# State update of a chunked linear attention by head: 48-column k v products on their own output partitions, two 48 x 48 quarters of the identity for the state so far

## The chip, the cores and the metric

The kernel runs on one core of a Trainium2 chip. The metric is the device time of one execution in microseconds (us); the median over runs is compared. Five engines work side by side, each through its own list of instructions: TensorE (PE, with its loads of weights as PEld), VectorE (DVE), ScalarE (ACT), GpSimd (POOL) and SyncE (SP), which issues most of the transfers (DMA). TensorE's clock is granted at one of two levels, 2.4 GHz or half of that; the profile gives it as a share of full speed.

## What is computed

Three layers in a row; the change is in the first, a linear attention with a decaying state per head (4 batches, 8 heads, 768 steps, 48 features):

```python
for t in range(S):
    cur = np.einsum('bhd,bhe->bhde', u[None] * kt, vt)
    y[:, :, t] = np.einsum('bhd,bhde->bhe', rt, state + cur)
    state = w[None, :, :, None] * state + np.einsum('bhd,bhe->bhde', kt, vt)
```

Then each of the 3072 tokens goes to one of 8 experts (ReLU, 384 to 1024 to 384), and then through a gated layer (384 to 1536 to 384) behind an RMS norm.

## The kernel before

The attention works on blocks of 128 steps: `n = 0 .. 23` is chunk `c = n // 4` of batch `b = n % 4`. One turn of the main loop is an iteration n. The last chunk (n = 20 to 23) needs no new state; the first (n = 0 to 3) has no old one. PE, DVE and ACT run in the order in which the code is written; the orders of POOL and SP are chosen by a scheduler when the program is built.

On PE an iteration with an old state holds, in this order: `scores(n + 1)` (L322: k by r, 48 features contracted, the two heads of a pair on input partitions 0 to 47 and 64 to 111), `xtrans(n - 1)` (L372), then in `attend(n)` the weighted v of the step itself (L333), r by the state (L335), `logits(n - 1)` (L383), scores by v (L343: 128 weight columns, 48 streamed columns, per head), and the new state (L358, L360). A matmul in float32 is two PE instructions, so the trace counts twice as many as the code writes. In the first chunk L333, L335 and L358 are missing, and L346 stands behind L343. Up to n = 5 a few matmuls of ones (`busy`, L99) are put in between.

The new state is made like this. Two heads share a pair `g` of 96 columns. The k of a block, decayed by `decayk` (L281), lies in one of five buffers `kdb` with each head padded from 48 to 64 columns, the pad zeroed once by POOL (L266). L360 multiplies 112 weight columns of a pair (48 + 16 zeros + 48) by 96 columns of v, so that a 112 x 96 block comes out: two 48 x 48 blocks that are wanted (a head's k by its own v) and two that are not. L358 adds the old state ahead of it, through a 112 x 112 identity. L363 on DVE multiplies by `w128`, which holds the decay over 128 steps for the wanted blocks and zero for the others; `w128` is made once from `pw` and a mask of two columns `hm` (L243, L244, L530).

The routing of the tokens (`route`) runs once per four blocks in pieces; the second piece begins on PE with L439, between L335 and L383, and waits for `cums`, the last of a row of small DVE instructions (L408 to L427) that begins one iteration earlier.

The loads of a block to come are issued by SP; that of v waits until L360 of the block that used the buffer is done (four buffers).

Of the kernel before, what the change touches and what calls it, by code (L numbers as in the profile page):

```python
# [7 lines left out]
F32 = mybir.dt.float32  # L8
# [5 lines left out]
ALU = mybir.AluOpType  # L14
AX = mybir.AxisListType

P = 128
# [7 lines left out]
HP = 64  # L25
# [21 lines left out]
def bcast(ap, shape):  # L47
    return ap.to_broadcast(shape)
# [3 lines left out]
def fused_kernel(  # L52
# [130 lines left out]
    with tc.tile_pool(name="at1", bufs=1) as at1, \  # L183
# [58 lines left out]
        hm = at1.tile([PP, 2], F32, name="hm")  # L242
        nc.vector.tensor_scalar(hm[:, 0:1], pidx[:PP], float(D), None, op0=ALU.is_lt)  # L243
        nc.vector.tensor_scalar(hm[:, 1:2], pidx[:PP], float(HP), None, op0=ALU.is_ge)  # L244


# [17 lines left out]
        kdb = [at1.tile([P, H, HP], F32, name=f"kdb{i}") for i in range(5)]  # L264
        for t in kdb:
            nc.gpsimd.memset(t[:, :, D:], 0.0)  # L266
# [11 lines left out]
        def decayk(n):  # L278

            kd[n] = kdb[n % 5]  # L280
            (nc.vector if n < 2 else nc.gpsimd).tensor_tensor(  # L281
                kd[n][:, :, :D], rkin[n][:, DM:].rearrange("p (h d) -> p h d", h=H), ftab, op=ALU.mult)
# [44 lines left out]
        def attend(n, between):  # L327
# [25 lines left out]
            if c < NCH - 1:  # L353
                s = st[b] if c > 0 else at1.tile([PP, G, PD], F32, name=f"s{b}")
                sf = s.rearrange("p g e -> p (g e)")
                if c > 0:

                    nc.tensor.matmul(pkv[:PP, :DM], ident[:PP, :PP], sf, start=True, stop=False, skip_group_check=True)  # L358
                for g in range(G):
                    nc.tensor.matmul(pkv[:PP, g * PD:(g + 1) * PD],  # L360
                                     kd[n].rearrange("p h d -> p (h d)")[:, g * 2 * HP:g * 2 * HP + PP],
                                     vv[:, g * PD:(g + 1) * PD], start=(c == 0), stop=True, skip_group_check=True)
                nc.vector.tensor_tensor(sf, pkv[:PP, :DM], w128.rearrange("p g e -> p (g e)"), op=ALU.mult)  # L363
                st[b] = s
# [163 lines left out]
        w128 = at1.tile([PP, G, PD], F32, name="w128")  # L528
        for j in range(2):
            nc.vector.tensor_tensor(w128[:, :, j * D:(j + 1) * D],  # L530
                                    bcast(pw[:, 7, :].unsqueeze(2), [PP, G, D]),
                                    bcast(hm[:, j:j + 1].unsqueeze(1), [PP, G, D]), op=ALU.mult)
# [633 lines left out]
```

## Time and profile before

| what | value |
|---|---|
| median of 3 runs | 923.24 us (922.04 to 928.17) |
| the profiled execution | 925.68 us, its span 923.9 us |
| PE busy | 892.5 us, 97% of the span |
| DVE busy | 505.1 us, 55% |
| ACT busy | 350.8 us, 38% |
| POOL busy | 278.5 us, 30% |
| TensorE clock granted, mean | 0.972 |

The attention takes the first 200 us or so of the span, and the rest is the two layers behind it. PE's share of busy time is high all through, and its matmuls overlap each other, so the share alone does not say which instruction is worth what. For that the chain of work that ended last is read, in which an entry reaches from its own start to the start of the next entry.

### The profile page before, as it was taken

Reading aid. Unit: us, or ns where it says so; the run is one execution under the profiler, and the core shown is the slowest. Engines: PE = TensorE matmul, PEld = TensorE weight load, DVE = VectorE, ACT = ScalarE, POOL = GpSimd, SP = SyncE. Lnnn points to the kernel's source line nnn. Section 1 sums busy time; section 2 is a strip of 40 time slices with the busy share of each in tenths; the row PEclk is TensorE's granted clock in tenths of the full one; section 3 lists DMA queues with packets and bytes.
Section 4 is the critical chain, followed back from the end, with each engine's and each line's share of the span. In section 5 each row is a group of like instructions: output and inputs, shape, how many; then the busy total and the mean of one; then the engine's idle time right before and its main releaser. Section 6 shows DMA issues by size and latency. Waiting matters only on the chain.

```text
span 923.9 us, 12722 instructions
## 1 busy us (share of the span) xinstructions
PE 892.5 (97%) x4912; PEld 783.3 (85%) x4912; DVE 505.1 (55%) x887; ACT 350.8 (38%) x742; POOL 278.5 (30%) x250
## 2 busy tenths in 40 slices
PE   7899999979999999999999999999999999999997
PEld 4788888848999999998878778888888888888886
DVE  6457798755677777877579843422432242233102
ACT  1435546544444544455443422322322142241211
POOL 6446697630000000103312132132123123124121
PEclk8789979988999999999999999999999999999999
DMA  6579866444675566533321000000000000000000
GB/s 181 156 234 284 252 198 198 137 154 131 203 244 180 188 203 209 178 126 104 137 69 50 19 35 1 1 16 19 0 1 35 1 1 35 1 0 35 1 1 34
DMA packets 34263, 93.55 MB, mean 101 GB/s; under 512 B 4368, under 2 KB 12584, under 8 KB 34200
## 3 DMA queue, kind: packets, MB, share of 16 engines
q1 hardware_dynamic: 23976, 53.53, 18.9%
q0 software_dynamic: 8928, 33.83, 11.4%
q10 hardware_dynamic: 1296, 5.35, 1.5%
q8 instruction: 39, 0.64, 0.3%
q14 instruction: 24, 0.20, 0.1%
HBM read 73.19 MB, written 19.50 MB: 100 GB/s over the span
## 4 chain that ended last, share of the span: by engine, by line
PE 80%; DVE 9%; issue 4%; ACT 3%; DMA 2%; POOL 1%; SPq 0%; POOLq 0%; DVEq 0%; ACTq 0%
PE ph L955 11%; PE px L343 5%; PE p2o L619 4%; PE p2o L617 4%; PE p2o L618 4%; PE pg L618 4%; PE pv L619 4%; PE pv L617 4%; PE pv L618 4%; PE pg L619 4%; PE pg L617 4%; PE po L617 4%; PE po L618 4%; PE po L619 4%; PE pa L322 3%
## 5 line engine op out<-in xcount | busy, mean ns | idle before, releaser
L1061 POOL TENSOR_TENSOR l<-sg,h 128x512 fp32r<-128x512 f32 x69 | 92.2, 1336 | 305.2 <-ACT h L1060 303.8
L1051 DVE TENSOR_TENSOR sg<-sg,pv 128x512 f32<-128x512 f32 x72 | 49.4, 686 | 236.7 <-PE pv L619 224.2
L619 PE MATMUL p2o<-hi_o,l 128*128 128x384 f32 x276 | 93.4, 338 | 3.2 <-POOL l L1061 3.2
L1050 ACT ACTIVATE sg<-pg 128x512 f32<-128x512 f32 x72 | 42.9, 596 | 139.7 <-PE pg L619 137.4
L617 PE MATMUL p2o<-hi_o,h 128*128 128x384 f32 x276 | 93.2, 338 | 1.3 <-ACT h L1060 1.3
L618 PE MATMUL p2o<-lo_o,h 128*128 128x384 f32 x276 | 92.7, 336 | 0.0
L1060 ACT CAST h<-sg 128x512 fp32r<-128x512 f32 x69 | 42.9, 621 | 130.7 <-DVE sg L1051 130.7
L617 PE MATMUL pv<-nh,hi_v 128*128 128x512 f32 x216 | 85.3, 395 | 0.9 <-ACT sg L1050 0.9
L618 PE MATMUL pg<-nl,hi_g 128*128 128x512 f32 x216 | 85.1, 394 | 0.5 <-DVE nl L904 0.5
L619 PE MATMUL pv<-nh,lo_v 128*128 128x512 f32 x216 | 85.2, 395 | 0.0
L618 PE MATMUL pv<-nl,hi_v 128*128 128x512 f32 x216 | 85.2, 395 | 0.0
L617 PE MATMUL pg<-nh,hi_g 128*128 128x512 f32 x216 | 85.2, 394 | 0.0
L619 PE MATMUL pg<-nh,lo_g 128*128 128x512 f32 x216 | 85.1, 394 | 0.0
L120 POOL DMA_DIRECT2D raw_w<-in_w_dram x25 | 19.0, 760 | 180.9 <-DVE hl L957 83.7
L955 PE MATMUL ph<-xh,hi_w 128*128 128x432 f32 x192 | 70.3, 366 | 1.8 <-DVE hl L957 1.4
L955 PE MATMUL ph<-xh,lo_w 128*128 128x432 f32 x192 | 69.8, 364 | 0.0
L955 PE MATMUL ph<-xl,hi_w 128*128 128x432 f32 x192 | 69.5, 364 | 0.0
L617 PE MATMUL po<-hh,hi_w 128*128 128x432 f32 x192 | 69.5, 362 | 0.0
L619 PE MATMUL po<-hh,lo_w 128*128 128x432 f32 x192 | 68.8, 358 | 0.0
L618 PE MATMUL po<-hl,hi_w 128*128 128x432 f32 x192 | 68.8, 358 | 0.0
L137 DVE TENSOR_TENSOR lo_w<-raw_w,hi_w 128x768 fp32r<-128x768 f32 x54 | 49.3, 955 | 19.9 <-ACT hi_w L133 19.9
L617 PEld LDWEIGHTS p2o<-hi_o,h 128*128 128x128 f32 x276 | 51.8, 188 | 5.3 <-ACT h L1060 2.1
(208 smaller groups left out, 1890.7 us busy)
## 6 DMA issues: line engine op xcount, KB each, us to landing
raw_w<-in_w_dram POOLq DMA_DIRECT2D x25, 768.0 KB, 5.4
rkTb<-in_rkt_dram SPq DMA_DIRECT2D x48, 192.0 KB
rk<-in_rkv_dram SPq DMA_DIRECT2D x24, 384.0 KB
raw_w<-in_w_dram SPq DMA_DIRECT2D x7, 768.0 KB
xs<-zt ACTq DMA_DIRECT2D x6, 770.0 KB
v<-in_rkv_dram SPq DMA_DIRECT2D x24, 192.0 KB
craw_g<-in_m2g_dram SPq DMA_DIRECT2D x9, 512.0 KB
craw_v<-in_m2v_dram SPq DMA_DIRECT2D x9, 512.0 KB
```

What stands on the lines that cost most here:

```text
L120: ld = self.queue.dma_start(raw.rearrange("p (a n) -> p a n", a=src.shape[1]), src)
L137: eng.tensor_tensor(lo[:, t], raw[:, t], hi[:, t].bitcast(F32), op=ALU.subtract)
L322: nc.tensor.matmul(pas[j][:, g, :], kT[n][t, g, :], rT[n][t, g, :], start=True, stop=True)
L343: nc.tensor.matmul(px[:, h * D:(h + 1) * D], am[n][:, h, :], vv[:, h * D:(h + 1) * D], start=(c == 0 and h == 0), stop=(c > 0), skip_group ...
L617: nc.tensor.matmul(ps, a[0], b[0], start=first, stop=False)
L618: nc.tensor.matmul(ps, a[0], b[1], start=False, stop=False)
L619: nc.tensor.matmul(ps, a[1], b[0], start=False, stop=last)
L955: nc.tensor.matmul(ph[:, :CAP], wp[:, o:o + P], xp[:, i, :CAP], start=(j == 0), stop=(j == len(parts) - 1))
L1050: nc.scalar.activation(sg, pg, AF.Silu)
L1051: nc.vector.tensor_tensor(sg, sg, pv, op=ALU.mult)
L1060: nc.scalar.copy(hh, sg)
L1061: (nc.vector if kept else nc.gpsimd).tensor_tensor(hl, sg, hh.bitcast(F32), op=ALU.subtract)
```

## The change

The five `kdb` buffers lose their pads, and POOL's five memsets of them go. Each head gets its own matmul: 48 weight columns by 48 streamed columns, written to output partitions 0 to 47 for the first head of a pair and 64 to 111 for the second. The result of a block is 48 partitions by 4 x 48 columns for each half, 192 columns where there were 384. The old state is added by two matmuls of a 48 x 48 quarter of the identity, on input and output partitions 0 to 47 and 64 to 111, with 192 streamed columns each. DVE multiplies each half by the decay, read from `pw` with a step of zero, and writes only the wanted blocks of the state; the unwanted blocks are zeroed once, by four memsets of 112 x 384 on POOL. `hm` and `w128` are gone.

```diff
-        hm = at1.tile([PP, 2], F32, name="hm")
-        nc.vector.tensor_scalar(hm[:, 0:1], pidx[:PP], float(D), None, op0=ALU.is_lt)
-        nc.vector.tensor_scalar(hm[:, 1:2], pidx[:PP], float(HP), None, op0=ALU.is_ge)
...
-        kdb = [at1.tile([P, H, HP], F32, name=f"kdb{i}") for i in range(5)]
-        for t in kdb:
-            nc.gpsimd.memset(t[:, :, D:], 0.0)
+        kdb = [at1.tile([P, H, D], F32, name=f"kdb{i}") for i in range(5)]
+
+        states = [at1.tile([PP, G, PD], F32, name=f"s{b}") for b in range(B)]
+        for t in states:
+            nc.gpsimd.memset(t, 0.0)
+        halves = [(slice(j * HP, j * HP + D), slice(j * D, (j + 1) * D)) for j in range(2)]
...
-                kd[n][:, :, :D], rkin[n][:, DM:].rearrange("p (h d) -> p h d", h=H), ftab, op=ALU.mult)
+                kd[n], rkin[n][:, DM:].rearrange("p (h d) -> p h d", h=H), ftab, op=ALU.mult)
...
-                s = st[b] if c > 0 else at1.tile([PP, G, PD], F32, name=f"s{b}")
-                sf = s.rearrange("p g e -> p (g e)")
+                s = st[b] if c > 0 else states[b]
+                kv = pkv[:, :G * D].rearrange("p (g e) -> p g e", g=G)
                 if c > 0:
 
-                    nc.tensor.matmul(pkv[:PP, :DM], ident[:PP, :PP], sf, start=True, stop=False, skip_group_check=True)
+                    for r, e in halves:
+                        nc.tensor.matmul(kv[r], ident[r, r], s[r, :, e], start=True, stop=False, skip_group_check=True)
                 for g in range(G):
-                    nc.tensor.matmul(pkv[:PP, g * PD:(g + 1) * PD],
-                                     kd[n].rearrange("p h d -> p (h d)")[:, g * 2 * HP:g * 2 * HP + PP],
-                                     vv[:, g * PD:(g + 1) * PD], start=(c == 0), stop=True, skip_group_check=True)
-                nc.vector.tensor_tensor(sf, pkv[:PP, :DM], w128.rearrange("p g e -> p (g e)"), op=ALU.mult)
+                    for j, (r, e) in enumerate(halves):
+                        nc.tensor.matmul(kv[r, g, :], kd[n][:, 2 * g + j, :],
+                                         vv[:, (2 * g + j) * D:(2 * g + j + 1) * D],
+                                         start=(c == 0), stop=True, skip_group_check=True)
+                for r, e in halves:
+                    nc.vector.tensor_tensor(s[r, :, e], kv[r], bcast(pw[r, 7, :].unsqueeze(2), [D, G, D]), op=ALU.mult)
...
-        w128 = at1.tile([PP, G, PD], F32, name="w128")
-        for j in range(2):
-            nc.vector.tensor_tensor(w128[:, :, j * D:(j + 1) * D],
-                                    bcast(pw[:, 7, :].unsqueeze(2), [PP, G, D]),
-                                    bcast(hm[:, j:j + 1].unsqueeze(1), [PP, G, D]), op=ALU.mult)
```

On PE, an iteration of the third chunk, before (from the transposes of `xtrans` to the next iteration's scores; `x4` stands for four matmuls in a row):

```order
L372 MATMUL pxT_1143<-ident,x_930 128x128 x3
L333 MATMUL px_1150<-qv_1097,ident 128x384
L335 MATMUL px_1150<-s_522,rkTb_114 128x96 x4
L383 MATMUL pxT_1143<-wr,xT_1147 128x16 x3
L343 MATMUL px_1150<-v_785,am_1048 128x48 x8
L358 MATMUL pkv_1179<-s_522,ident 112x384
L360 MATMUL pkv_1179<-v_785,kdb_189 112x96 x4
L322 MATMUL pa_0_1221<-rkTb_112 128x128
```

The same place in the change, whose line numbers differ by a few:

```order
L373 MATMUL pxT_1198<-ident,x_967 128x128 x3
L331 MATMUL px_1205<-qv_1146,ident 128x384
L333 MATMUL px_1205<-s_193,rkTb_114 128x96 x4
L384 MATMUL pxT_1198<-wr,xT_1202 128x16 x3
L341 MATMUL px_1205<-v_816,am_1097 128x48 x8
L357 MATMUL pkv_1234<-s_193,ident 48x192 x2
L360 MATMUL pkv_1234<-v_816,kdb_186 48x48 x8
L320 MATMUL pa_0_1282<-rkTb_112 128x128
```

Nothing moves past anything else there: one matmul of 384 columns becomes two of 192, and four of 96 become eight of 48, in the same place.

On DVE, from the masking of the first block's scores to the first new state, before (`am` are masked scores, `q` sums of r u k, `rkTb` the decayed r and k by feature):

```order
L324 TENSOR_TENSOR am_213<-pa_1_215,smask 128x4x128
L527 TENSOR_TENSOR pw<-pw 112x4
L530 TENSOR_TENSOR w_228<-pw,hm 112x4x48 x2
L534 TENSOR_SCALAR iota_231<-rowi 128x8
L536 MEMSET cum_233 128x4
L281 TENSOR_TENSOR kdb_188<-rk_146,ftab 128x8x48
L293 TENSOR_REDUCE q_246<-ru_236 128x8
L309 TENSOR_TENSOR rkTb_113<-rkTb_113,decays 112x1024
L324 TENSOR_TENSOR am_265<-pa_0_266,smask 128x4x128
L324 TENSOR_TENSOR am_265<-pa_1_267,smask 128x4x128
L363 TENSOR_TENSOR s_312<-pkv_298,w_228 112x384
```

The same stretch in the change:

```order
L322 TENSOR_TENSOR am_213<-pa_1_215,smask 128x4x128
L528 TENSOR_TENSOR pw<-pw 112x4
L530 TENSOR_SCALAR iota_228<-rowi 128x8
L532 MEMSET cum_230 128x4
L279 TENSOR_TENSOR kdb_185<-rk_146,ftab 128x384
L291 TENSOR_REDUCE q_243<-ru_233 128x8
L307 TENSOR_TENSOR rkTb_113<-rkTb_113,decays 112x1024
L322 TENSOR_TENSOR am_262<-pa_0_263,smask 128x4x128
L322 TENSOR_TENSOR am_262<-pa_1_264,smask 128x4x128
L364 TENSOR_TENSOR s_190<-pkv_295,pw 48x4x48 x2
```

The two products that made `w128` are gone, and the update of the state is two instructions of 48 x 192 where it was one of 112 x 384; the rest stands as it stood.

## Rows read from the trace of the kernel before

**Rows 1.** Busy us by stretch: length, PE, PEld, DVE, ACT, POOL, clock, DMA share, GB/s

```profile
17.00:53.00 36.00, 33.18 (x221) 27.46 (x221) 15.21 (x24) 13.15 (x51) 17.57 (x18) 0.74 0.48 144
53.00:122.00 69.00, 69.00 (x602) 61.36 (x601) 53.37 (x109) 37.10 (x135) 42.54 (x35) 1.00 0.83 254
122.00:142.00 20.00, 19.22 (x127) 16.64 (x128) 16.09 (x33) 8.93 (x30) 15.53 (x15) 0.74 0.65 202
```

**Rows 2.** Chain that ended last, iteration 11 (start us, us, what)

```profile
101.14 1.09 PE pa L322 x16
...
102.71 0.65 PE px L333 x2
...
104.82 1.81 PE px L343 x16
106.64 0.70 PE pkv L358 x2
107.34 0.77 PE pkv L360 x8
108.11 1.09 PE pa L322 x16
```

**Rows 3.** The same chain in the first chunk and at half clock

```profile
21.69 0.78 PE pkv L360 x8
...
39.44 1.47 PE pkv L360 x8
...
129.26 1.39 PE pkv L358 x2
130.64 1.47 PE pkv L360 x8
132.11 2.01 PE pa L322 x16
...
141.90 1.09 PE pa L322 x16
...
161.85 1.22 PE pkv L358 x2
```

**Rows 4.** Groups of PE by form, first 225 us

```profile
L360 PE MATMUL pkv<-v,kdb 128*112 128x96 f32 x160 | 22.4, 292 | 0.0
...
L358 PE MATMUL pkv<-s,ident 112*112 112x384 f32 x32 | 15.1, 555 | 0.0
```

**Rows 5.** PE's instructions at 101 us and at 230 us (start us, us, instruction)

```profile
100.68 0.46 PE L360 MATMUL pkv<-v,kdb 128*112 128x96 f32 x3
101.06 0.38 PE L322 MATMUL pa<-rkTb 48*128 48x128 f32 x2
...
229.72 0.36 PE L918 MATMUL pt<-ident,xg 108*4 108x54 f32 x4
230.01 0.47 PE L617 MATMUL po<-hh,hi_w 128*128 128x432 f32 x1
```

**Rows 6.** Groups of DVE by form, first 225 us

```profile
L324 DVE TENSOR_TENSOR am<-pa,smask 128x512 f32<-128x512 f32 x48 | 30.9, 684 | 6.1 <-PE pa L322 5.7
...
L363 DVE TENSOR_TENSOR s<-pkv,w 112x384 f32<-112x384 f32 x20 | 11.1, 557 | 38.8 <-PE pkv L360 38.8
```

**Rows 7.** All engines in order of time, before the first iteration

```profile
10.72 0.99 POOL L287 TENSOR_TENSOR ru<-rk,ub 128x384 f32<-128x384 f32 x1 [4.33 <-DMA ub<-in_u_dram]
...
13.57 3.57 PE L99 MATMUL pa<-ones 128*128 128x512 bf16 x8 [3.48 <-DVE am L324]
```

**Rows 8.** All engines in order of time, a routing's counts and PE behind them

```profile
95.00 0.36 DVE L427 TENSOR_TENSOR cums<-cums,ohb 128x8 bf16<-128x8 bf16 x2
...
96.97 0.18 PE L439 MATMUL prk<-cums,ones 128*128 128x32 bf16 x1
...
125.92 0.18 PE L439 MATMUL prk<-cums,ones 128*128 128x32 bf16 x1 [0.78 <-DVE cums L427]
```

**Rows 9.** Who waited for whom from 53 to 115 us (us in total, times, longest)

```profile
DVE s L363 <- PE pkv L360: 12.0, 7, 3.6
```

## The prediction

> **What bounds the kernel now.** I read the busy times by stretch first. From 53 to 122 us PE is busy in all 69 us at the full clock, while DVE has 53.4 us, POOL 42.5, ACT 37.1, and the DMA engines a share of 0.83 [rows 1]. PE is the limit of that stretch, but two resources stand close behind it. In the stretches around it (17 to 53, 122 to 142) the granted clock is 0.74, so part of the time PE ran at 1.2 GHz.
>
> Then the chain that ended last, which tells what a PE instruction is worth. In a steady iteration it is PE alone from scores to scores: 101.14 to 108.11, or 6.97 us [rows 2]. The state takes 0.70 us (L358) and 0.77 us (L360) of it, together 1.47. At half clock the same two take 1.39 and 1.47 [rows 3]. L360 stands there 20 times (160 instructions by 8) and L358 16 times (32 by 2) [rows 4]. So at most some 30 us of the kernel's 925 can be touched.
>
> What sets a PE instruction's time shows in three rows of the iteration. L333 streams 384 columns in 0.325 us, 0.85 ns a column. L343 streams only 48 but loads 128 weight columns, and takes 0.113 us, 0.88 ns a weight column. L360 has 112 weight columns and 96 streamed, and takes 0.096 us, that is the larger of 0.098 and 0.082, not their sum [rows 2]. So the time is the larger of loading and streaming. L322 loads and streams 128 columns and should take 0.109 by that, yet 16 of them take 1.09 us, 0.068 each [rows 2]: the two heads, which use different input partitions (0 to 47, 64 to 111), run at the same time.
>
> **The change, part by part.**
>
> *L360, new.* 16 instructions per block, each 48 weight columns (0.042 us) and 48 streamed (0.041). In a row they take 16 x 0.042 = 0.67 us; if the two output halves run in pairs, 0.34. The trace of before has no two matmuls on different output partitions side by side. Its nearest row for a thin output is L918 (4 output columns, 54 streamed): four start at 229.72 and the next matmul at 230.01, so 0.073 each at most with the change of shape behind them in it [rows 5]. That shows that thin instructions can follow each other this fast. The bounds are 0.34 and 0.67. I take 0.34, because the row nearest to it is L322, where halves of the array do run in pairs.
>
> The Trainium skill ("TensorE: Matmul & The Clock Gate", Part 3, Measured speedup vs the span model) gives 2.38 times for three column tiles of 32. Two tiles by the same share would have 1.59 times, an estimate from that page: 0.42 us for L360 and 0.41 for the old state, and with the changes of shape below a gain of 0.46 per block instead of 0.62. No row here shows it.
>
> *Old state, new.* Four instructions of 192 streamed columns: 0.163 each, 0.65 in a row, 0.33 in pairs (both input and output halves differ), against 0.70 now. I take 0.33.
>
> *Changes of the array's shape.* From L360 to L322 the last three L360 take 0.38 us to the next start, where three take 0.29 otherwise [rows 2, 5]: 0.09 for going from the whole array to halves. Before, an iteration has two such changes (into and out of L322). The new one has two more, into the quarters and from them to the column halves: +0.18.
>
> So a block at full clock takes 0.34 + 0.33 + 0.18 = 0.85 instead of 1.47: -0.62, and +0.03 if nothing runs in pairs. At half clock by the same columns (L360's 0.184 for 96 streamed gives 0.092; L358's 0.695 for 384 gives 0.35): 8 x 0.092 + 2 x 0.35 + 0.2 = 1.64 instead of 2.86, -1.2 [rows 3]. In the first chunk three blocks go from 1.47 to 0.94 and one from 0.78 to 0.52, with two more changes of shape as well: -1.85. Of the 16 blocks with an old state, two were at half clock in this trace, at 129.26 and 161.85 [rows 3]. The sum: 14 x 0.62 + 2 x 1.2 + 1.85 = 12.9 us off PE.
>
> *DVE, per block.* One product of 384 columns took 0.557 us; the 512 of L324 take 0.684, so 1.0 ns a column and 0.17 fixed [rows 6]. Two of 192 cost 0.73: +0.17. What hides it: DVE waited 12.0 us for L360 in seven of the nine iterations from 53 to 115 [rows 9]. If that cover were gone, the masked scores queued behind it would be 0.17 late per block, 3 us in all. Below nothing isn't possible, since two instructions replace one of the same length.
>
> *The start.* `w128` and `hm` go from DVE, but PE is covered there by eight matmuls of ones, 3.57 us from 13.57 [rows 7]; gain zero. POOL's memsets change from 5 small ones to 4 of 384 columns, ahead of an idle 4.33 us that ends with a transfer [rows 7]: zero. POOL's order also swaps two products of the first blocks, in the same cover; without it the first weighted v would be 1 us late, once. The product of k in `decayk` has the same 384 elements.
>
> *What comes back.* PE now reaches a routing's L439 earlier by two blocks' gain, 1.24 us. At 96.97 the counts had been ready since 95.36, 1.6 us ahead; at 125.92 PE waited 0.78 us for them [rows 8]. DVE's row starts from PE's own logits and so moves too, but not where DVE is full. I charge one such wait, +1.2. And behind that wait the clock fell: the iteration from 132.11 to 141.90 took 9.79 us instead of 6.97, and its neighbours share it [rows 1, 3]. The new iteration has the same waits with less work between them. I charge one more iteration at half clock, +2.8. The DMA share of 0.83 at 6.97 us an iteration becomes 0.91 at 6.35; since the loads are issued an iteration or more ahead, I charge nothing.
>
> So 12.9 - 4.0 = 8.9 us: the profiled 925.7 becomes 916.8. That execution is 2.4 us above the median of the runs, 923.24; for a median I state 915.0.
>
> **The rivals.**
>
> *A, the forecast:* the halves run in pairs and the chain keeps most of the gain. Speaks for it: L322. 908 to 921 by one or two half-clock iterations more or fewer than charged. Chance 0.60.
>
> *B, the change doesn't do what it says:* two column halves are served one after the other. Then a full-clock block is +0.03, a half-clock one 1.47 + 1.4 + 0.2 against 2.86, +0.2, and the first chunk up to +0.2 per block, together about +1.5: 925 as a median. For it: no row has two column halves together; L322's pairs differ in input partitions, these don't. Chance 0.20.
>
> *C, in pairs, but the time goes elsewhere:* the shorter iteration meets the routing on DVE (routing iterations fill DVE: 16.1 of 20 us from 122 to 142) and the clock falls in three iterations more than before, two above the one charged, with one more wait: 915 + 2 x 2.8 + 1.2 = 922. For it: the clock stood at 0.74 on both sides of the dense stretch [rows 1]. Against it: at 53 to 122 there is no wait at all. Chance 0.13.
>
> *D, slower:* the loads of weights are not hidden any more, so that each thin instruction pays loading plus streaming: 16 x 0.083 + 4 x 0.205 + 0.18 = 2.33 instead of 1.47, +0.86 in 16 blocks, and about +0.8 in the first four: +17, or 940. It decides from about 0.6 us per block on, i.e. if more than two thirds of a load stays bare. Against it: L360 now hides its streaming behind its loads (0.096, not 0.18). The Trainium skill ("TensorE: Matmul & The Clock Gate", Part 3, What overlaps and what doesn't) says that a load overlaps matmuls in flight only where the row groups differ; by that rule D would hold, since the column halves share all rows. The trace of before speaks against the rule, by the same L360, whose instructions share all rows too. Chance 0.05.
>
> **How the numbers follow.** The runs and the comparison tell about 1% from no change, which is 9.2 us, so "faster" means below 914.0. A's own range is cut there a little below its middle: 0.33 faster, 0.27 same. B (0.20) and nearly all of C (0.13) are the same. D (0.05) and 0.02 for something not thought of are slower. Faster 0.33, same 0.60, slower 0.07. The range reaches down to a little below A's end (907, fewer half-clock iterations than before) and up to B's end with the spread of the runs (928).
>
> **What would show it.** In the profile after, the chain's entries for the new L357 and L360 at full clock: 0.42 and 0.43 with the changes of shape, if A; 0.75 each, if B; above 0.9 and 1.4, if D. The steady iteration of 6.97 would be 6.35 under A and C, 7.0 under B. C shows in the granted clock from 122 to 180 us and in waits of PE for `cums`. DVE's update would be two instructions near 0.36 us. The forecast is wrong if the entries of the state are short and the end is still not earlier: then the gain went into waits or the clock, and if pairs don't form at all, its main term is gone.

## The result and the profile after

The change made the kernel slower: median 935.76 us (933.75 to 956.21, 6 runs) against 922.64 us (917.32 to 930.23, 6 runs) of the kernel before, a ratio of 1.0148 with an interval of 1.0100 to 1.0196. The forecast was 915.0 us with a range up to 928, so it was wrong in sign and in range. (Ratios here leave out executions in which the chip was disturbed; medians contain them.)

| | before | change |
|---|---|---|
| profiled execution | 925.68 us | 936.19 us |
| its span | 923.9 us | 934.2 us |
| TensorE clock granted, mean | 0.972 | 0.949 |
| span times mean clock | 898.0 us | 886.6 us |
| span less that | 25.9 us | 47.6 us |

The last two rows are worked out, and they are the key to the case. Span times mean clock is the span as it would be if the same time on PE's clock had all passed at 2.4 GHz; I call it clocked time. It fell by 11.4 us. What is left, the time that the lower level cost, rose by 21.7. The difference of the two is the 10.3 us by which the span grew. Clocked time is not pure work: over 113 executions of the kernel before it runs from 893 to 902 us, and falls by some 0.23 us for each us that the lower level cost (an estimate, a line laid through these executions). By that, 5 of the 11.4 us would come with the lower clock alone.

First the work itself. PE in order of time, in a steady iteration of the change (start us, us, instruction). L357 is the old state, L360 the k v products, L320 the scores of the next block:

```profile
105.98 0.53 PE L357 MATMUL pkv<-s,ident 48*48 48x192 f32 x4
106.44 0.56 PE L360 MATMUL pkv<-v,kdb 128*48 128x48 f32 x16
106.93 1.16 PE L320 MATMUL pa<-rkTb 48*128 48x128 f32 x16
```

From start to start the state takes 0.46 + 0.49 = 0.95 us where it took 1.47 [rows 2]. Steady iterations, from scores to scores, go from 6.97 to 6.45 us, by the same 0.52. At half clock the same two took:

```profile
126.45 0.88 PE L357 MATMUL pkv<-s,ident 48*48 48x192 f32 x4
127.26 0.88 PE L360 MATMUL pkv<-v,kdb 128*48 128x48 f32 x16
128.07 2.08 PE L320 MATMUL pa<-rkTb 48*128 48x128 f32 x16
```

0.81 + 0.81 = 1.62 us, where it was 2.86 [rows 3]. On DVE the update of the state is two instructions of 0.354 us (groups of DVE by form, the first 225 us; busy us, then mean ns):

```profile
L364 DVE TENSOR_TENSOR s<-pkv,pw 48x192 f32<-48x192 f32 x40 | 14.2, 354 | 36.6 <-PE pkv L360 36.2
```

Now the clock. Both kernels cut at the same places of the program: start, scores of block 1, scores of block 6, scores of block 21, first matmul of the experts, end. Columns are length, PE, PEld, DVE, ACT, POOL, clock, DMA share, GB/s. Before:

```profile
0.00:17.10 17.10, 11.01 (x47) 4.49 (x47) 12.59 (x44) 2.04 (x5) 10.77 (x20) 0.84 0.80 207
17.10:58.90 41.80, 38.98 (x268) 32.66 (x267) 17.46 (x26) 16.65 (x64) 18.35 (x18) 0.78 0.54 162
58.90:171.80 112.90, 111.89 (x925) 98.76 (x924) 91.46 (x184) 57.94 (x206) 81.17 (x67) 0.94 0.77 233
171.80:212.40 40.60, 32.09 (x243) 24.76 (x242) 23.29 (x105) 19.56 (x64) 16.12 (x15) 0.88 0.40 130
212.40:923.90 711.50, 698.52 (x3437) 622.66 (x3437) 360.31 (x530) 254.60 (x404) 152.06 (x130) 1.00 0.22 73
```

The change:

```profile
0.00:16.60 16.60, 11.40 (x45) 4.61 (x45) 12.32 (x41) 2.20 (x6) 10.25 (x19) 0.90 0.84 208
16.60:60.90 44.30, 41.28 (x310) 32.73 (x309) 17.98 (x29) 16.32 (x64) 19.05 (x19) 0.69 0.51 151
60.90:176.70 115.80, 111.42 (x1078) 97.02 (x1076) 96.91 (x199) 58.05 (x207) 77.19 (x66) 0.87 0.74 229
176.70:222.50 45.80, 36.69 (x243) 28.66 (x241) 25.37 (x105) 19.48 (x64) 15.41 (x15) 0.76 0.36 115
222.50:934.20 711.70, 700.28 (x3437) 624.63 (x3437) 360.62 (x530) 254.73 (x404) 152.12 (x130) 0.99 0.22 73
```

Length times one less the clock gives what the lower level cost in each stretch: first blocks 9.2 before and 13.7 now; dense stretch 6.8 and 15.1; last blocks and routing 4.9 and 11.0; the rest, by difference from the totals, 5.0 and 7.8. The loss grew in every stretch but the start (2.7 us before, 1.7 now), and two of them have new waits.

In the last blocks, whose PE instructions the change does not touch, the same work takes 5.2 us more. What moved there is the order of POOL, which the scheduler chose anew: the change has the last block's product r u k (L286) behind scatters of routed tokens (L499). POOL and DVE in order of time, and below the dots PE:

```profile
183.80 1.01 POOL L499 DMA_INDIRECT xs<-x,pos  x1 [9.63 <-ACT x L490]
...
188.80 1.00 POOL L286 TENSOR_TENSOR ru<-ru,rk 128x384 f32<-128x384 f32 x1
189.83 0.55 DVE L291 TENSOR_REDUCE q<-ru 128x8 f32<-128x384 f32 x1 [1.88 <-POOL ru L286]
...
195.78 0.91 PE L331 MATMUL px<-qv,ident 128*128 128x384 f32 x2 [0.97 <-ACT qv L300]
```

Before, the same product stood ahead of these scatters:

```profile
174.22 2.08 POOL L288 TENSOR_TENSOR ru<-ru,rk 128x384 f32<-128x384 f32 x1
```

DVE waits 1.88 us for the late product, ACT 3.04 us for DVE's row behind it, and PE 0.67 and 0.97 us for ACT; the scores by v behind that wait take 3.54 us, at half clock, where before, with no such wait, they took 1.91.

The dense stretch also has new idle time: PE is idle for 4.4 us of it (115.80 less 111.42), before for 1.0. One wait is the largest. All engines in order of time, at 111 us of the change:

```profile
111.61 1.28 POOL L151 TENSOR_TENSOR lo_w<-raw_w,hi_w 128x512 fp32r<-128x512 f32 x1
111.86 4.01 DVE L307 TENSOR_TENSOR rkTb<-rkTb,decays 112x1024 f32<-112x1024 f32 x1
112.83 1.00 POOL L279 TENSOR_TENSOR kdb<-rk,ftab 128x384 f32<-128x384 f32 x1
113.80 0.98 POOL L285 TENSOR_TENSOR ru<-rk,ub 128x384 f32<-128x384 f32 x1
114.86 1.86 POOL L286 TENSOR_TENSOR ru<-ru,rk 128x384 f32<-128x384 f32 x1
...
115.97 2.17 PE L320 MATMUL pa<-rkTb 48*128 48x128 f32 x16 [2.51 <-issue]
```

DVE's product of the decayed r and k (L307), 1.21 us at its shortest, takes 4.01 while POOL runs product after product; it ends at 115.87, and PE's scores, which read it, start 0.1 us later after 2.51 idle. POOL is held too: its last product takes 1.86 us there, against 0.98 to 1.03 for the others of that size. The profile names no releaser ("issue"), so this reading was a guess at that point, and was tested.

### The profile page after: what moved, and what is told of

Read it like the earlier page. It is cut to its first block, busy times and chain, and to the rows that moved or that the text cites. A ratio compares the mean times of both kernels' runs of the same rounds, so it can differ in the third digit from the quotient of the medians.

```text
span 934.2 us, 13133 instructions
## 1 busy us (share of the span) xinstructions
PE 901.1 (96%) x5104; PEld 787.7 (84%) x5104; DVE 513.2 (55%) x903; ACT 350.8 (38%) x742; POOL 274.0 (29%) x249
## 4 chain that ended last, share of the span: by engine, by line
PE 67%; DVE 5%; issue 3%; ACT 2%; DMA 1%; POOL 1%; POOLq 0%; SPq 0%; ACTq 0%; DVEq 0%
PE ph L951 11%; PE pg L614 5%; PE pv L615 4%; PE pv L613 4%; PE pv L614 4%; PE pg L615 4%; PE p2o L615 4%; PE pg L613 4%; PE p2o L613 4%; PE p2o L614 4%; PE po L613 4%; PE po L615 4%; PE po L614 4%; PE pt L912 1%; DVE oraw L663 1%
```

## The experiments

Theory 1: the change saves PE what was forecast, and the clock takes back more, for two reasons: PE's time holds less that keeps the clock up, and DVE, stretched by POOL, makes PE wait. Its rivals: the pairs are to blame, for the clock or by their shape; or PE has simply too little to do; or DVE has too much work for shorter iterations. Summary (span and clock are those of the profiled execution, and not given for two kernels):

| kernel | median us | ratio to before (interval) | span, clock, clocked time |
|---|---|---|---|
| the change | 935.76 | 1.0148 (1.0100 to 1.0196) | 934.2, 0.949, 886.6 |
| e1, both fillers | 924.92 | 1.0026 (0.9988 to 1.0064) | 918.0, 0.974, 894.1 |
| e2, thin fillers | 976.73 | 1.0513 (1.0476 to 1.0551) | 979.1, 0.907, 888.0 |
| e3, pairs apart | 936.24 | 1.0140 (1.0088 to 1.0192) | 933.7, 0.956, 892.6 |
| e4, before, both fillers | 922.63 | 0.9972 (0.9941 to 1.0004) | |
| e5, middle filler | 937.48 | 1.0153 (1.0061 to 1.0245) | 933.3, 0.954, 890.4 |
| e6, e5 + first chunk | 937.50 | 1.0134 (1.0044 to 1.0223) | 933.6, 0.958, 894.4 |
| e7, e5 + k decay on DVE | 924.86 | 1.0032 (0.9988 to 1.0075) | 927.8, 0.954, 885.1 |
| e8, e5 + column halves | 930.48 | 1.0032 (0.9991 to 1.0073) | 927.7, 0.959, 889.7 |
| e9, k decay on DVE | 933.63 | 1.0178 (1.0116 to 1.0239) | 924.2, 0.960, 887.2 |
| e10, e1 + e6 + e7 | 921.96 | 1.0027 (0.9985 to 1.0069) | 919.0, 0.972, 893.3 |
| e11, before, k decay on DVE | 920.31 | 1.0008 (0.9960 to 1.0056) | 918.4, 0.977, 897.3 |
| e12, e11 + first chunk | 914.91 | 0.9939 (0.9902 to 0.9976) | 913.8, 0.981, 896.4 |
| e13, change, r u k left out | 924.06 | 1.0007 (0.9944 to 1.0071) | 915.8, 0.965, 883.7 |
| e16, e13 + k decay on DVE | 919.49 | 0.9951 (0.9906 to 0.9996) | 916.7, 0.965, 884.6 |
| e14, e10 + more in the first chunk | 914.62 | 0.9905 (0.9859 to 0.9952) | 907.2, 0.987, 895.4 |
| e15, before + first chunk | 914.48 | 0.9925 (0.9893 to 0.9957) | 913.5, 0.983, 898.0 |
| e17, e14 + column halves | 920.01 | 0.9869 (0.9817 to 0.9920) | |
| e18, e17, middle filler only | 911.27 | 0.9865 (0.9826 to 0.9903) | 909.6, 0.981, 892.3 |

### What holds the clock: e1, e2, e4

Both kernels put matmuls of ones (512 columns, L99) ahead of the scores and in the middle of scores by v, up to block 5. e1 does so up to block 19; e2 puts a float32 matmul of one streamed column at the same places; e4 is e1's edit in the kernel before.

```diff
-            busy(..., NBUSY[4] if n < NFILL else 0)
+            busy(..., NBUSY[4] if n < NT - B else 0)
...
-                if h == H // 2 and n < NFILL:
+                if h == H // 2 and c < NCH - 1:
```

> The change, with the two matmuls of ones (128 x 512, 0.21 us each at full clock) that stand in the first six iterations put into all twenty that make a state: one ahead of the scores, one in the middle of scores by v. Clock theory (the change takes busy work out of PE, and the granted clock falls more often and stays down longer): the time at half clock in the attention falls from some 58 us to below 40, and the time from 936 to 920 to 930, although PE gets 6 us of extra work. Waiting theory (PE is held by VectorE's late products of r and k by the decay, and the clock is only a follower): the long waits ahead of the scores (0.4, 2.5, 1.5 us) stay or shrink a little, the extra work adds up to 6 us, 934 to 942.

> The change, with the same two places filled from iteration 6 on by a thin float32 matmul each (128 weight columns loaded, one column streamed, two instructions, about 0.21 us), so that an iteration is as long as in the filled kernel but PE streams nothing more. Clock theory: no help, the clock falls as often or more often, 936 to 946. Waiting theory: VectorE gets 0.4 us more per iteration, the waits shrink, same as the filled kernel within 3 us.

> The kernel before, with the same two matmuls of ones in all twenty iterations: the control for the filled kernel. Clock theory: half-clock time falls here too, from some 37 us to 25 or less, 915 to 923. Waiting theory: 6 us of extra work, 923 to 930.

Busy times by stretch of e1:

```profile
53.00:122.00 69.00, 67.23 (x690) 57.35 (x689) 60.28 (x113) 35.29 (x129) 45.15 (x38) 0.98 0.84 264
122.00:177.00 55.00, 54.76 (x573) 47.03 (x572) 51.62 (x116) 34.16 (x120) 43.19 (x37) 1.00 0.62 194
```

and of e2:

```profile
53.00:122.00 69.00, 69.00 (x564) 59.65 (x564) 38.54 (x89) 25.95 (x94) 27.47 (x26) 0.72 0.70 220
122.00:177.00 55.00, 55.00 (x376) 47.25 (x374) 28.93 (x69) 21.32 (x71) 32.26 (x28) 0.59 0.44 128
```

In e2 PE is busy in all of both stretches and waits for nothing, and yet the clock stands at 0.72 and 0.59; filled with wide matmuls it stands at 0.98 and 1.00, with 1.8 us of waits in the first. So "PE has too little to do" falls. e1 has 7.5 us more clocked time than the change and is 11 us faster. Not all of that is the fillers': with e1's edit the scheduler puts POOL's last products ahead of the scatters again, the waits in the last blocks are gone, and these lose 4.6 us to the lower level instead of 11.0. In the dense stretch, where both kernels wait, the loss goes from 15.1 to 2.2. In the kernel before the same fillers buy nothing that can be told from no change (e4): from 53 to 122 us it stood at 1.00 already [rows 1].

Filling is not free: steady iterations are 6.92 us in e1, 0.47 above the change, so nearly all of the saving is spent on holding the clock. The filler in the middle alone costs 0.15 of it (6.60, e5).

### Are the pairs to blame: e3, e8

e3 writes the eight products of the first half, then those of the second, so that neighbours share output partitions:

```diff
-                for g in range(G):
-                    for j, (r, e) in enumerate(halves):
+                for j, (r, e) in enumerate(halves):
+                    for g in range(G):
```

> The change, with the eight k v products in another order: the four heads of the first output half, then the four of the second, so that neighbours share their output partitions. If neighbours on different output halves do run in pairs in the change, the 16 instructions take about 0.7 us instead of 0.36 and the steady iteration 6.8 instead of 6.45 us. Clock theory: PE is busy with more of its time again, fewer falls, 925 to 934. Waiting theory: the longer iteration gives VectorE 0.35 us, about the same, 928 to 936. If the pairs are not what shortens the iteration: 6.45 again, 936.

PE in order of time, in e3:

```profile
104.77 0.53 PE L357 MATMUL pkv<-s,ident 48*48 48x192 f32 x4
105.22 0.78 PE L360 MATMUL pkv<-v,kdb 128*48 128x48 f32 x16
105.93 1.16 PE L320 MATMUL pa<-rkTb 48*128 48x128 f32 x16
```

The products take 0.71 us apart and 0.49 in pairs, so pairs are real and worth 0.22 us a block, less than the 0.33 that I gave them. The time of the kernel is the same as the change's: 6 us more clocked time (892.6), a higher clock (0.956), no gain and no loss.

e8 (with the middle filler of e5, as e6 and e7) makes the old state by pieces of the identity that span all 112 input partitions, so that the array goes from column halves to column halves:

```diff
-                        nc.tensor.matmul(kv[r], ident[r, r], s[r, :, e], ...)
+                        nc.tensor.matmul(kv[r], ident[:PP, r], s[:, :, e], ...)
```

> The kernel with one filler, and the old state added by column halves of the identity with all 112 rows (two matmuls of 112 x 48 weights) instead of 48 x 48 quarters, so that one change of the array's shape per iteration goes. If a change of shape costs 0.09 us: the steady iteration is 0.09 us shorter than with one filler, 6.57 us, and 1 to 1.5 us in all. If the quarters' pairs need the separate rows: the old state takes 0.65 instead of 0.33 us, the iteration 6.9, and 4 to 6 us slower.

```profile
85.87 0.53 PE L357 MATMUL pkv<-s,ident 112*48 112x192 f32 x4
86.23 0.53 PE L360 MATMUL pkv<-v,kdb 128*48 128x48 f32 x16
86.69 1.16 PE L320 MATMUL pa<-rkTb 48*128 48x128 f32 x16
```

0.36 + 0.46 = 0.82 where the change has 0.95: the quarters cost 0.13 us a block that column halves don't. Steady iterations go from 6.60 (e5) to 6.47. The Trainium skill ("TensorEngine Tiling (Array Packing)", Key Properties) says that a change of the tiling mode drains the engine; this agrees with it in kind. The median went from 937.48 to 930.48, more than the 2 us of work, but the intervals overlap (1.0061 to 1.0245 and 0.9991 to 1.0073), so the two are not surely told apart.

### Fillers in part, and where k is decayed: e5, e6, e7, e9, e11

e5 has only the middle filler, up to block 19. e6 adds to it, in the first chunk, two fillers ahead of the logits and one more in the middle. e7 adds to e5 that VectorE decays every k, at the end of an iteration. e9 does that alone, without fillers, and e11 in the kernel before.

```diff
-            (nc.vector if n < 2 else nc.gpsimd).tensor_tensor(
+            nc.vector.tensor_tensor(
...
-                if n != -2:
+                if n in (-3, -1):
                     decayk(n + 3)
...
+            if 2 < n + 2 < NT:
+                decayk(n + 2)
```

> The change, with only one of the two extra matmuls of ones, that in the middle of scores by v (128 x 512, 0.21 us), in all twenty iterations that make a state; ahead of the scores it stands in the first six as before. The steady iteration should be 6.66 us, between the change (6.45) and both fillers (6.92). If PE's streaming around the scores by v is what the clock hangs on: no fall in the dense stretch but behind waits, and 919 to 926, 4 us under the two fillers at best. If one filler is not enough: falls as in the change, 928 to 938.

> The kernel with one filler, and in the first chunk (iterations 0 to 3, at half clock for most of the time in every kernel so far) more of them: two in the middle, and two in front of the logits, where PE waits 0.57 us for the transposed block anyway. Clock theory: the first four iterations go from some 9.3 us to 6.5 to 7.5 us each at full clock, 6 to 10 us faster than with one filler alone, 910 to 918. If those iterations are held by something other than the clock: no gain, or 2 us slower for the extra work.

> The kernel with one filler, and the product of k and the decay of all blocks on VectorE at the end of the iteration (0.55 us each) instead of on GpSimd (1.0 us each). It asks whether VectorE's late product of r and k by the decay (up to 4.0 us instead of 1.2 when GpSimd runs without a break) is what PE waited for. If so: those products take 1.2 to 2.0 us, the waits ahead of the scores (2.5, 1.5 us in the change, 1.8 us with two fillers) go, and the time is 2 to 6 us below that of one filler. If VectorE is simply full: its extra 0.55 us per iteration makes the waits longer, 2 to 6 us above.

> The change with the decayed k of all blocks made on VectorE, at the end of an iteration, and no filler (the run with the middle filler and the same move gained 12.6 us on the one without it). Theory 1, GpSimd's products of the size 128 x 384 stretch VectorE's product of r and k, so PE waits for its scores and the clock falls behind that wait: the waits at 116.0 and 167.3 us of the change (2.5 and 1.5) are below 1 us, span times granted clock stays that of the change (886.6), the clock rises from 0.949 to 0.963 or more, the time is 920 to 925. Theory 2, the clock falls for the thin pairs alone, whatever PE waits for: as the change, 932 to 938, clock 0.95.

> A control: the kernel before with the decayed k on VectorE. Theory 1: its PE waits only 0.8 us for VectorE between 53 and 180 us, so there is little to win, span times clock stays 897, clock 0.972 to 0.978: 917 to 924. Theory 2, the move itself is worth the 12 us that it brought the changed kernel, whatever the state does: 908 to 914.

e5 gains nothing on the change. Its dense stretch has waits still (1.62 us at 123.3 for a routing's counts, with two iterations at or near half clock behind), but lost only 5.4 us there. The larger loss of the profiled execution is in the last blocks, 22.0 us (clock 0.61 from 165.9 to 222.4), where the one wait of PE from 166 us to the fall is of 0.21 us. e6 and e7 show the same (20.9 and 22.7 us); what brings it on stays open. e6 clears the first chunk (iterations 2 and 3 take 7.25 and 6.74 us where e5 has 9.03 and 11.45); besides the last blocks it loses 8.0 us in the dense stretch, most of it behind a wait of 3.40 us. Its rows, DVE and PE in order of time:

```profile
118.27 3.78 DVE L428 TENSOR_TENSOR ohb<-oh,m 128x32 bf16<-128x32 f32 x1
...
123.53 0.18 PE L442 MATMUL prk<-cums,ones 128*128 128x32 bf16 x1 [3.40 <-DVE cums L430]
```

A product of 32 elements, 0.19 us otherwise, took 3.78 while POOL ran three products from 118.83 to 121.99. e7's median is 12.6 us below e5's (the intervals overlap a little, 1.0061 and 1.0075), and I took POOL's product of k for the culprit, although the product of r and k still took up to 2.94 us in e7, not 2.0 as expected. e9 says no: with the same move and no filler the change stays at 933.63. Its rows at 119 us:

```profile
119.02 2.85 DVE L426 TENSOR_TENSOR ohb<-oh,m 128x32 bf16<-128x32 f32 x1
...
119.58 1.29 POOL L151 TENSOR_TENSOR lo_w<-raw_w,hi_w 128x512 fp32r<-128x512 f32 x1
...
128.49 2.17 PE L320 MATMUL pa<-rkTb 48*128 48x128 f32 x16 [2.03 <-issue]
```

The product of r and k takes 2.02 us at most in e9, so that much the move did. But a routing's product is held while POOL runs the weight split (above) and r u k: the row is 2.7 us late, what is queued behind it too, and PE waits 2.03 us at the scores. So e9's waits (2.03 and 1.36) are no smaller than the change's (2.51 and 1.50), and the expectation of theory 1 for it was wrong: it had named one instruction of POOL's where others do as well. In the kernel before the move alone brings nothing (e11).

### What makes PE wait: e13, e16

Blocks 3 to 23 share the sums of block 3, so POOL's two products of r u k are left out for 20 blocks; the routing then sends the tokens otherwise. DVE's and PE's instructions stay. e16 has the move of k too.

```diff
+            if n > 3:
+                ruk[n] = ruc
+                return
+            ru = ruc if n == 3 else at2.tile([P, DM], F32, tag="ru", name=f"ru_{n}")
             nc.gpsimd.tensor_tensor(ru, rkin[n][:, :DM], ub, op=ALU.mult)
```

> The change without GpSimd's two products r u k for 20 of 24 blocks: blocks 3 to 23 all use the sums of block 3, so the output differs from the reference and the routing too. VectorE's and TensorE's work is unchanged, no filler. GpSimd loses some 2.2 us of every iteration. Theory 1, VectorE's instructions are stretched by GpSimd's products (1.2 to 4.0 us, 0.2 to 2.9 us) and PE's waits at the scores come from that: no wait above 0.5 us at the scores between 53 and 180 us, the longest product of r and k below 2 us, clock 0.965 or more, time 915 to 923. Theory 2, VectorE has too much work for iterations of 6.45 us whatever GpSimd does: waits of 1.5 to 2.5 us remain, time 931 to 937.

> The same with the decayed k on VectorE too, so that GpSimd has only a weight split in two of three iterations and the scatters. It leaves out the same products r u k. Theory 1: the same as without the move or better, no wait above 0.5 us, clock 0.965 or more, 913 to 922. Theory 2, VectorE's load (0.55 us more of it per iteration) sets the waits: longer ones, 934 to 940.

DVE's product of r and k from 53 to 180 us, in the change and in e13:

```profile
L307 DVE TENSOR_TENSOR rkTb<-rkTb,decays 112x1024 f32<-112x1024 f32 x17 | 34.9, 2055 | 0.0
```

```profile
L311 DVE TENSOR_TENSOR rkTb<-rkTb,decays 112x1024 f32<-112x1024 f32 x18 | 28.6, 1591 | 0.0
```

and who waited at the scores in the same stretch (us in total, times, longest), in the change:

```profile
PE pa L320 <- issue: 4.0, 2, 2.5
```

In e13 PE has no such row: its weight loads wait twice there, 0.4 us at most, and PE is busy in all of 53 to 177 us. The longest product is 2.92 us, not below 2 as expected, but none is late. With POOL's products gone the waits are gone, though DVE's work is the same; and e16, which gives DVE more work, does no worse: PE is busy in all of 53 to 177 us there too. So DVE's load is not the cause, POOL beside it is. Nor did DVE wait for POOL's results: in the change's list of waits from 53 to 180 us no instruction of DVE waits for one of POOL's. (By which path POOL holds DVE the trace does not show.) The Trainium skill ("SBUF — State Buffer", SBUF: two separate sides) has the two engines share a pair of ports that one holds for a whole instruction while the other is blocked; the rows agree in kind, but DVE lost more than the one POOL product of 1.0 to 1.3 us that this text speaks of: 2.8 us at 111.86 (the change) and 3.6 at 118.27 (e6).

What e13 says of the clock shows when it is cut at the same places; these are the first blocks, the dense stretch and the last blocks:

```profile
16.50:63.20 46.70, 43.68 (x310) 34.92 (x309) 18.28 (x29) 16.15 (x64) 11.60 (x11) 0.65 0.49 145
63.20:163.80 100.60, 100.60 (x1080) 88.31 (x1076) 79.13 (x199) 57.77 (x207) 40.25 (x36) 0.97 0.85 256
163.80:204.20 40.40, 32.50 (x244) 24.50 (x242) 24.69 (x106) 19.32 (x64) 13.39 (x13) 0.90 0.47 151
```

The dense stretch loses 3.0 us (15.1 in the change, 6.8 before) and the last blocks 4.0 (11.0 and 4.9), with steady iterations of 6.45 us and no filler. So in these two the saved PE work alone does not bring the clock down; the waits do. The first reason of theory 1 falls there. What is left lies in the first chunk, 16.3 us (iterations 1 to 4 take 11.4, 11.4, 9.1 and 9.2 us), and in one more place, iterations 14 and 15, where the clock falls without a wait of PE. The first chunk's loss differs much between profiled executions in which its PE instructions are those of the change: 10.8 us in e1 and e5, 13.7 in the change and e8, 16.3 in e13 and e16. The kernel before lost 9.2 there, and 11.9 in e11. So what the change costs in the first chunk can't be told from one execution of each.

### The first chunk, and the best versions: e10, e12, e14, e15, e17, e18

e10 is e1, e6 and e7 together; e14 puts more fillers ahead of the first chunk's logits (eight for block 1, then four); e17 has e8's column halves too; e18 is e17 without the filler ahead of the scores from block 6 on. e15 is the kernel before with e6's first chunk, e12 that with k decayed on VectorE.

```diff
+            if c == 0 and n > 0:
+                busy(px, 8 if n == 1 else 4)
             between()
...
-                    busy(pkv, NBUSY[5])
+                    busy(pkv, 2 if c == 0 else 1)
```

> The change with everything that held the clock in one run: both fillers in all blocks with a new state, three more in the first chunk, and the decayed k on VectorE. Theory 1: the shares add. Span times clock 894 (893.0 with both fillers, one more for the first chunk), clock 0.978 or more, so a span of 914 and a time of 916, with iterations of the first chunk below 8 us where they were 9 to 11.5. Theory 2: the rest of the lost clock comes back elsewhere, in the last blocks and behind them: 923 to 926.

> The kernel before with the decayed k on VectorE and the three more fillers per block in the first chunk, against which the run with everything is to be held. Theory 1, the change's own gain of some 10 us of clocked work is kept once the clock is held: this kernel takes 917 to 922, some 3 us above the changed one, for there the fillers eat most of the gain. Theory 2: first chunk and waits were the whole matter in both kernels, and this one takes 910 to 914.

> The run with both fillers, the decayed k on VectorE and more fillers in the first chunk, with these still more: eight of them ahead of the first logits and four ahead of the next two, where PE waited 1.39 us and then ran two iterations at half clock. Theory 1: the first chunk goes at the full clock (iterations 2 and 3 near 7 us instead of 11.8 and 7.3), span times clock 894.5, clock 0.978, time 916. Theory 2, the clock falls there in any case: 921 to 923.

> A control: the kernel before with only the more fillers in the first chunk, without the move of the decayed k. Of the 8 us or so that both together won, theory 1 gives most to the first chunk (half clock there 17 us down to 5, so 6 us): 916 to 919. Theory 2, the move wins it, by the waits at 125.9 us and behind: 919 to 923.

> The run with the most fillers, and the old state by 112 x 48 pieces of the identity over all input partitions (two changes of the array's shape less; 0.13 us an iteration less in the run with the middle filler). Clocked work 893.5 where it was 895.3. Theory 1: the clock stays at 0.98, time 911 to 914, some 2 us below the same without this and below the kernel before with the first chunk filled (914.5). Theory 2: the two microseconds go to the clock again: 914 to 918.

> The same without the filler ahead of the scores from block 6 on: steady iterations of 6.5 us instead of 6.8, clocked work about 889.5. Theory 1, PE's filled time holds the clock and only the waits lose it: with the products of k on VectorE there are waits of 1 to 2 us left, so the clock falls two or three times and stands at 0.965 to 0.972, time 917 to 923, slower than with the filler. Theory 2, the first chunk was the larger part of the loss: clock 0.977, 912.

The stretch from 17 to 53 us in the change, in e15 and in e14:

```profile
17.00:53.00 36.00, 32.98 (x247) 25.71 (x247) 15.16 (x26) 12.59 (x49) 16.23 (x17) 0.68 0.48 140
```

```profile
17.00:53.00 36.00, 34.47 (x275) 28.24 (x273) 18.77 (x25) 16.54 (x64) 19.01 (x18) 0.93 0.60 186
```

```profile
17.00:53.00 36.00, 35.83 (x357) 27.89 (x353) 25.88 (x39) 16.29 (x63) 16.30 (x14) 1.00 0.72 217
```

The kernel before was at 0.74 there [rows 1]. So the first chunk was a loss in both kernels that a few fillers mend: e15, with nothing else, is at 914.48, and e12 adds nothing to it. In e10 the same number of fillers did not do for the changed kernel (iterations 1 and 2 still at 9.72 and 11.83 us, where e6, filled alike, had 10.52 and 7.25), in e14 more of them did (8.01 and 6.72). Theory 1 had put e10 at 916 and e12 at 917 to 922; they took 921.96 and 914.91, so it was wrong for both.

e14 can't be told from e15 (0.9905 and 0.9925): 895.4 of clocked time against 898.0, so the fillers eat most of the saving. e17's runs spread from 908.56 to 924.51, and its ratio of 0.9869 fits the first theory's 911 to 914; it can't be told from e14. e18 was expected at 917 to 923 by theory 1, for the waits that were still there. It took 911.27, with all six runs between 910.93 and 917.06. Its waits are there (PE in order of time, and busy times by stretch):

```profile
105.25 1.25 PE L320 MATMUL pa<-rkTb 48*128 48x128 f32 x16 [1.21 <-issue]
```

```profile
53.00:122.00 69.00, 66.45 (x734) 60.40 (x733) 66.51 (x140) 38.97 (x137) 41.29 (x35) 1.00 0.90 271
```

PE was idle for 2.5 us of that stretch and the clock stood at 1.00 all through. So a wait of 1.2 us need not cost the clock. Its length alone does not decide: in e8, which has the middle filler too, the scores behind a wait of 1.82 us took 1.25 us, at full clock, and in e6 those behind one of 1.04 us took 1.98. Theory 1 made waits too much of a trigger, and the filler ahead of the scores kept nothing that can be told (ratios 0.9869 with it, 0.9865 without). e18 has the lowest median, 1.35% below the kernel before (interval 0.97 to 1.74). Its distance to e15, 3.2 us, is from two comparisons whose intervals overlap; that the changed state is worth that much once the clock is held is not shown.

## Why the prediction was wrong, step by step

**PE is the limit, and the state is 1.47 us of an iteration.** Right: every steady iteration became shorter by what the state became shorter.

**L360 in pairs.** Right in kind, a little too good: 0.49 with the change of shape where I had 0.43. Pairs bring 0.22 (e3). Rival B is out, and so is D: the sixteen instructions share all rows of the array and took 0.49 us in all, where bare loads would have made it over 1.3. The Trainium skill's rule that only loads into other row groups overlap ("TensorE: Matmul & The Clock Gate", Part 3, What overlaps and what doesn't) does not hold here by that row.

**Old state and changes of shape.** 0.46 where I had 0.42. The changes are 0.13 us a block dearer than column halves would be (e8). At half clock 1.62 against a forecast of 1.64.

**The sum off PE.** 12.9 us forecast. With the entries measured the same sum is 14 x 0.52 + 2 x 1.24 + 2.3 = 12.1, where 2.3 us is the first chunk's, from the start of L360 to the scores (2.03 to 1.35 three times, 1.08 to 0.81 once). Mis-sized by the 0.1 us per block, and no more.

**DVE and the start.** 0.36 us an instruction forecast, 0.354 measured. The first scores of block 1 came at 16.6 us instead of 17.1; nothing was lost there. But the prediction looked at POOL's order for the first blocks alone and put it at nothing; it was the order in the last blocks that cost.

**What comes back.** This step failed. I charged 4.0 us; 21.7 came back as clock. Three things were wrong in it. The wait was looked for at the routing's counts, with 1.2 us; it came at the scores, 2.51 and 1.50 us, and at the counts of the dense stretch there was none. I had read DVE's 53.4 of 69 us [rows 1] as room. Part of that time was DVE held by POOL: the product of r and k has a mean of 1.80 us in the kernel before and a shortest of 1.21, which a look at the spread of one instruction's durations would have told. Second, POOL's order in the last blocks was left out, and PE waited 0.67 and 0.97 us there. Third, the clock was charged as one more iteration at half clock, 2.8 us. Behind these waits the dense stretch lost 8.3 us more than before, and the last blocks 6.1 more. That the waits and not the saved work did it is shown for the dense stretch by e13 and e16, which save the same and lose 3.0 us there. For the last blocks it rests on the chain of waits in the trace and on e1, e13 and e16, whose POOL has the products early or not at all and which lose 4.0 to 4.6 us there; no run changed the order alone. The other 7.3 us, 4.5 of them in the first chunk, stay open.

**The rivals.** C named the mechanism in kind (in pairs, but the time goes to waits and clock), though not the place of the waits, and was priced at 922 with three iterations. It came nearly 14 us dearer, and so ended on the slower side, to which I had given 0.07. What the profile showed and I did not weigh: a clock of 0.74 on both sides of the dense stretch [rows 1] meant that the attention ran near the lower level in much of its time outside that stretch, so nothing bounded C at three iterations.

## What to carry to other kernels

Where the granted clock is below 1 anywhere near, weigh a saving on PE in two numbers, clocked time and what the lower level costs, since the first can fall while the second rises by more. Look at the stretches that a change doesn't touch as well, and at the order of a queue that a scheduler fills, since a small edit can turn it round; here the cheapest gain (0.75%, some 7 us) was a handful of wide fillers in the first chunk of the kernel before. And before an engine's busy time is called room, compare the shortest and the mean duration of one of its instructions: what is stretched there is late for someone as soon as the iteration is shorter.

## What the runs showed of the hardware

- PE busy without a break is not enough for the full clock: with thin float32 work in the same places, iterations of some 10 us, clock 0.59 from 122 to 177 us and PE busy in all 55 us (e2), against 6.92 us and 1.00 with 512-column matmuls (e1).
- Two float32 matmuls on different output partitions that share all input partitions run in pairs: 16 of 48 x 48 in 0.49 us with the change of shape behind them, 0.71 when written so that neighbours share output partitions (e3).
- The old state through quarters of the array took 0.13 us a block more than through column halves (0.95 and 0.82 us, the change and e8).
- A DVE product of 32 elements on each partition took 3.78 us while POOL ran products one after the other (e6), twenty times its usual 0.19; the kernel before has one of 3.80 us too.
- The change's iterations of 6.45 us, without a filler and with PE busy throughout, held the full clock for 52 us (69 to 121 us of e13, clock 1.00), and lost it from 121 to 138 us (clock 0.80) with PE still busy throughout.
